# A fused attention and MLP kernel whose planner gets its first 400 operations as a list

## The chip, the cores and the metric

One NeuronCore of a Trainium2 chip runs the whole program. The metric is the device time of one execution in microseconds (us), given as the median of several runs. A profiled execution of the kernel before is shown beside them; every instant below counts from the first instruction of that profile.

## The reference

Two computations follow each other. First, attention with a causal window of 64 positions, over 8 batches, 8 heads, 576 positions and a head size of 64:

```
scores = q @ k.T / sqrt(64)                  # only 0 <= i - j < 64 counts
attn   = exp(scores - max) / (sum + 1e-9)
a      = attn @ v
```

Its result is laid out as x with 4608 tokens (8 x 576) of 512 features. Second, an MLP with a gate of its own:

```
h   = x @ w_in                               # 4608 x 2048
g   = h * clip(h + 3, 0, 6) / 6
out = g @ w_out                              # 4608 x 512, float32
```

## The kernel before

The MLP works on tiles of 512 tokens, 9 of them. Stage 1 of a tile makes 16 chunks of h, each of four 128x512 matmuls (`s1_part`, recorded as L736; one matmul for each pair of heads g, since x is made pair by pair); ScalarE (ACT) applies a relu with bias (L749) and VectorE (DVE) multiplies (L754). Stage 2 makes four output blocks of 128 tokens, each with 16 matmuls (`s2_part`, L775); ACT or DVE copies the finished block out of PSUM (`s2_close`, L788) and SyncE (SP) stores it.

Between those matmuls stands the attention of the next batch, so that x is ready when its tile begins. For a batch this is: the loads of q, k and v by GpSimd's DMA queue (POOL, L389); the turning of q and k so that the head size lies along partitions (for batches 0 and 1 on TensorE, `fold_pair` and `fold_two`, L513 and L539, with copies out of PSUM, L518 and L544; later by two DMA transposes on SP, `turn`, L391); the scores (L580; for batch 0 with a mask added by a matmul, L564), the exp on ACT (L596), the mask on DVE (L605); and the product with v. For batches 0 and 1 that product has the queries along partitions (`pv_rows`, L625), is divided by its row sum on DVE (L635, L636) and turned back by TensorE (`turn_x`, L651, then a copy, L368). For later batches (`pv`, L677) the sums come out as rows, and ACT makes the reciprocal as exp(-ln(sum)): two LN instructions (L683) and one EXP (L686) for each of five products of a batch (four pairs of heads and "e", the last 64 positions of all pairs). Two DVE multiplies (L697) then write x and free the PSUM bank.

v is wanted in two alignments. For batch 0, pairs 0 and 1 come through a float32 stage loaded by SP in four pieces of 128 positions, and six copies cast it to bf16 (`cast_v`, L368): for the blocks 0 and 1 the straight piece and two pieces shifted by 64 positions, then the same for blocks 2 and 3. Pairs 2 and 3 are loaded as bf16 by POOL (`load_vhead`), and `shift_v` (L456) makes the shifted parts. `copy_op` and `shift_v` may go to any of several engines.

Every engine takes its instructions in the order in which the program emits them, and that order comes from a planner that runs while the program is built. `Plan.add` notes each operation with a duration, its reads and writes; the operation's number (`op.seq`) is its place in that list. `Plan.solve` picks one operation after another, the one that could start first by its own account (a preference for each stream is subtracted), gives it an engine, a start and an end, and PSUM banks: there are five slots, two "n" of one bank, one "b" and two "a" of two banks. At the end all operations are emitted in the order of their planned starts. A result counts as usable by another engine `LAT` ns after the operation's end. For the first loads of each queue the planner doesn't work out the landing but takes it from the tables `LANDED` (SP, POOL, ACT) and `NEXT` (POOL's following ones):

```
op.done = max(op.land or ring[eng] + 600 + op.late, t + dur)
```

with `op.land` the entry of the table (for NEXT, plus `MARGIN`), t the planned issue and dur the issue's own duration. `COLD_PE` is the time up to which TensorE counts as 1.6 times slower. Matmuls on ones (L977) are put ahead of the first TensorE operation, as many as fit before its planned start.

The numbers that matter below:

| number | operation |
|---|---|
| 3, 5 / 10 | casts of q and k of pair 0 / ACT's table load |
| 11-19 | POOL: loads of q and k of the pairs 1 to 3 of batch 0, identity, mask |
| 20, 21 / 22, 23 | POOL: load_vhead, pairs 2 / 3 of batch 0 |
| 24, 25 | DVE: fold and ident, from the identity |
| 26, 27, 28 / 29, 30, 31 | cast_v, blocks 0-1 / 2-3: straight, shifted, shifted |
| 32-36 | POOL: the five loads of w_in (chunks 0-1, 2-3, 4-7, 8-11, 12-15) |
| 37-40 | shift_v of the pairs 2 and 3 |
| 85, 86, 91, 92 | POOL: the four loads of w_out |
| 88, 89 / 93, 94 | POOL: q and k of batch 1, pairs 0-1 / 2-3 |
| 162 | first TensorE operation that needs the last quarter of w_out |
| 203-210 | shift_v of batch 1 |
| 223, 227, 231 | pv_rows of batch 1, pairs 0, 1, 2 |
| 255, 256 | SP: turn of q, of k of batch 2 |
| 165, 167, 177, 179 | SP: the stores of the first four output blocks |
| 323, 329 | s2_close of the output blocks 5 and 6 |
| 353, 359, 365, 371, 377 | pv of batch 2: pairs 0, 1, e, 2, 3 |
| 354-356, 360-362, 366-368, 372-374, 378-380 | their LN, LN, EXP on ACT |
| 357-358, 363-364, 369-370, 375-376, 381-382 | their multiplies on DVE |
| 406-408 | first matmuls of tile 2's stage 1 (408 is the first on pair 3) |

## Time and profile before

| what | value |
|---|---|
| median of 3 runs (lowest, highest) | 300.72 us (300.55, 301.58) |
| the profiled execution: its own time, its span | 299.92 us, 298.2 us |
| granted TensorE clock | 0.999 |
| busy: TensorE (PE), DVE, ACT, POOL | 287.4, 198.6, 207.6, 121.7 us |
| POOL's DMA queue (q0) | 98816 packets, 17.80 MB |
| HBM read, written | 36.70 MB, 9.44 MB |

The span runs from the first to the last instruction; 1.72 us of the execution's time lie outside of it. Busy time of an engine counts instructions and not their waits on semaphores; matmuls are pipelined, and their ends are modelled, so consecutive starts tell more of TensorE than its busy share. "Released by" in a view is inferred from semaphores.

### The profile page before, as it was taken

The page shows a single profiled execution, that of the slowest core. Times are in us where ns is not written, and L with a number is a line of the kernel's source. Part 1 is how long each engine was busy: PE and PEld are TensorE (multiplying, and loading weights), DVE is VectorE, ACT ScalarE, POOL GpSimd, SP SyncE. Part 2 cuts the span into 40 slices and gives each one's busy share as a digit, 9 for nine tenths or more (in the row PEclk, how much of TensorE's full clock was granted, in tenths as well). Part 3 has the DMA queues.
Part 4 walks back from the last instruction along what each step waited for, and adds up shares of the span by engine and source line. Part 5 has one row for each costly group of instructions (what it writes and reads, how often), then busy time and mean ns, then how long its engine had stood idle before and what let it go on. Part 6 is the DMA issues. An engine that isn't in the chain of part 4 may idle for free.

```text
span 298.2 us, 6931 instructions
## 1 busy us (share of the span) xinstructions
PE 287.4 (96%) x2779; PEld 153.7 (52%) x2825; DVE 198.6 (67%) x326; ACT 207.6 (70%) x323; POOL 121.7 (41%) x171
## 2 busy tenths in 40 slices
PE   6899999999999999999999999999999999999996
PEld 6544545445544554455687554455445544444443
DVE  3778657786777975878678767878677868106700
ACT  3878665887968795778677958886787768227611
POOL 8884667059547906930991069405000000000000
PEclk9999999999999999999999999999999999999999
DMA  8999999989999999999996799969900110110011
GB/s 186 189 208 205 204 190 169 192 93 152 129 210 147 114 155 177 181 64 208 137 169 41 143 178 170 71 110 173 118 2 35 37 70 1 37 70 35 0 73 70
DMA packets 137680, 36.66 MB, mean 123 GB/s; under 512 B 126256, under 2 KB 132912, under 8 KB 137648
## 3 DMA queue, kind: packets, MB, share of 16 engines
q0 software_dynamic: 98816, 17.80, 73.9%
q1 hardware_dynamic: 38688, 18.12, 24.8%
q8 instruction: 22, 0.36, 0.5%
q10 hardware_dynamic: 144, 0.29, 0.4%
q14 instruction: 10, 0.08, 0.1%
HBM read 36.70 MB, written 9.44 MB: 155 GB/s over the span
## 4 chain that ended last, share of the span: by engine, by line
PE 82%; DMA 11%; POOL 4%; issue 2%; ACT 0%; POOLq 0%
PE pn L775 36%; PE pn L736 16%; PE pa L736 12%; PE pb L736 9%; DMA Ak<-in_k_dram 7%; DMA wout<-in_moe_w_out_dram 4%; PE pa L677 4%; PE pa L580 2%; PE pa L775 1%; POOL nq L389 1%; PE pb L677 1%; POOL nk L389 1%; POOL Aq L389 0%; POOL V L456 0%; PE pb L580 0%
## 5 line engine op out<-in xcount | busy, mean ns | idle before, releaser
L775 PE MATMUL pn<-wout,gT 128*128 128x512 bf16 x532 | 125.3, 379 | 2.2 <-issue 1.1
L736 PEld LDWEIGHTS <-win 128*128 128x128 bf16 x640 | 62.0, 98 | 60.5
L775 PEld LDWEIGHTS <-gT 128*128 128x128 bf16 x592 | 54.3, 98 | 57.7
L736 PE MATMUL pn<-xT,win 128*128 128x512 bf16 (+1 forms) x271 | 62.0, 357 | 0.3
L749 ACT ACTIVATE t<-pn,half 128x512 bf16<-128x512 f32 x62 | 42.7, 689 | 8.8 <-PE pn L736 8.5
L754 DVE SCALAR_TENSOR_TENSOR gT<-t,pa 128x512 bf16<-128x512 bf16 x47 | 32.2, 687 | 24.2 <-ACT t L749 23.9
L754 DVE SCALAR_TENSOR_TENSOR gT<-t,pn 128x512 bf16<-128x512 bf16 x62 | 42.6, 687 | 8.6 <-ACT t L749 8.4
L736 PE MATMUL pa<-xT,win 128*128 128x512 bf16 (+1 forms) x201 | 47.8, 358 | 0.3
L389 POOL DMA_DIRECT2D nk<-in_k_dram x55 | 41.8, 790 | 5.3 <-DMA Tk<-nk 4.6
L389 POOL DMA_DIRECT2D V<-in_v_dram x40 | 33.2, 848 | 14.4 <-PE pa L677 11.9
L749 ACT ACTIVATE t<-pa,half 128x512 bf16<-128x512 f32 x47 | 32.2, 686 | 8.9 <-PE pa L736 8.5
L697 DVE TENSOR_TENSOR xT<-pa,rec 64x512 bf16<-64x512 f32 (+1 forms) x48 | 32.0, 667 | 8.6 <-ACT rec L686 7.6
L736 PE MATMUL pb<-xT,win 128*128 128x512 bf16 (+1 forms) x153 | 36.3, 357 | 0.5 <-issue 0.5
L754 DVE SCALAR_TENSOR_TENSOR gT<-t,pb 128x512 bf16<-128x512 bf16 x35 | 24.0, 686 | 16.2 <-ACT t L749 16.1
L788 ACT COPY osb<-pn 128x512 f32<-128x512 f32 x17 | 10.0, 586 | 32.2 <-PE pn L775 32.2
L683 ACT ACTIVATE rec<-pa 64x512 f32<-64x512 f32 (+1 forms) x48 | 27.6, 574 | 4.8 <-PE pa L677 3.7
L749 ACT ACTIVATE t<-pb,half 128x512 bf16<-128x512 f32 x35 | 24.2, 690 | 7.6 <-PE pb L736 7.5
L389 POOL DMA_DIRECT2D nq<-in_q_dram x30 | 26.8, 892 | 3.3 <-DMA wout<-in_moe_w_out_dram 1.6
L596 ACT ACTIVATE pT<-pa 128x1024 bf16<-128x1024 f32 x25 | 24.6, 1021 | 1.5 <-PE pa L580 1.3
L605 DVE TENSOR_TENSOR pT<-pT,mask 128x1024 bf16<-128x1024 bf16 x28 | 18.9, 689 | 4.8 <-ACT pT L596 4.8
L677 PEld LDWEIGHTS <-V 128*128 128x128 bf16 x448 | 16.9, 98 | 6.8 <-DVE xT L697 0.5
L853 POOL COPY scrap<-Tq 128x1 bf16<-128x1 bf16 x5 | 0.9, 189 | 44.4 <-DMA Tq<-nq 44.4
(96 smaller groups left out, 205.9 us busy)
## 6 DMA issues: line engine op xcount, KB each, us to landing
out_dram<-osb SPq DMA_DIRECT2D x35, 256.0 KB, 3.6
V<-in_v_dram POOLq DMA_DIRECT2D x28, 128.0 KB, 5.9
nq<-in_q_dram POOLq DMA_DIRECT2D x24, 128.0 KB, 4.7
nk<-in_k_dram POOLq DMA_DIRECT2D x41, 64.0 KB, 4.2
wout<-in_moe_w_out_dram POOLq DMA_DIRECT2D x4, 512.0 KB, 14.5
win<-in_moe_w_in_dram POOLq DMA_DIRECT2D x3, 512.0 KB, 9.2
V<-in_v_dram POOLq DMA_DIRECT2D x12, 64.0 KB, 5.8
Aq<-in_q_dram POOLq DMA_DIRECT2D x2, 288.0 KB, 13.7
```

Of the source, the lines that this page charges most:

```text
L389: em = lambda: e.dma_start(out=out_ap, in_=in_ap)
L580: nc.tensor.matmul(to[o, home(b, g, h) if x == "e" else h, y * D : (y + 1) * D], lhsT=w, rhs=q_cols(b, r, g, j), start=not masked, stop=no ...
L596: nc.scalar.activation(out=p_[:].rearrange("p j h c -> p h j c"), in_=wide(add_far if masked else op, name)[:, :, 0 : n * D].rearrange("p ...
L605: nc.vector.tensor_tensor(out=pp, in0=pp, in1=mask[:, m0 : m0 + n, :, :].rearrange("p j h c -> p (j h c)"), op=MULT)
L677: nc.tensor.matmul(wide(op, name)[:, h, y * D : (y + 1) * D], lhsT=V[:, blk, g, h * D : h * D + P], rhs=p_[:, y, home(b, g, h) if end else ...
L683: add("ACT", act(n), lambda h=h: nc.scalar.activation(out=rc[rows[h], 0:n], in_=wide(op, name)[rows[1 - h], h, 0:n], func=LN), reads=[key] ...
L697: nc.vector.tensor_tensor(out=o, in0=a, in1=z, op=MULT)
L736: nc.tensor.matmul(bank(op, name)[:, to : to + n], lhsT=win16[:, g, fc * P : (fc + 1) * P], rhs=xT[:, g, o : o + n], start=(g == 0), stop= ...
L749: nc.scalar.activation(out=t1[ti][:], in_=bank(op, name), func=RELU, bias=half[:], scale=1.0 / 6.0)
L754: nc.vector.scalar_tensor_tensor(out=gT[:, fc, :], in0=t1[ti][:], scalar=1.0, in1=bank(op, name), op0=MIN, op1=MULT)
L775: nc.tensor.matmul(bank(op, name)[:, 0:n], lhsT=gT[:, fc, col : col + P], rhs=wout16[:, fc, js], start=(fc == 0), stop=(fc == NFC - 1))
L788: alts = {e: (f(n), (lambda e=e: cpy(e)(out=osb[oi][:, js], in_=bank(op, name)[:, 0:n])), False) for e, f in (("DVE", dve), ("ACT", act))}
```

## The change

It gives `Plan.solve` a list, `PLACE`, of 400 operation numbers. While fewer than 400 operations are placed, the next one of the list is the only candidate; where an operation may go to several engines, the next letter of `WHERE` (D, A, P for DVE, ACT, POOL) tells which. From the 401st on the planner picks as before. Besides: the tables `LANDED` and `NEXT` get other times, `MARGIN` goes from 300 to 0 and `COLD_PE` from 6500 to 4500; `LAT` becomes a table by the engine that made the result, with 20 for a landed DMA; the price of an ACT operation falls from 160 + n/1.2 to 75 + n/1.2 ns, that of a DVE copy within SBUF from 60 + 0.9 n to 60 + 0.73 n; and in `pv` both multiplies, not the last alone, count as holders of the PSUM bank.

```diff
--- before.py
+++ after.py
@@ -21,13 +21,34 @@
 
 WINDOW = 64
 LANDED = {
-    "SP": (3000, 6210, 8070, 8430, 9600),
-    "POOL": (4600, 6820, 7920, 9640, 10900, 11600, 11950, 12350, 12800, 13200),
-    "ACT": (3200,),
+    "SP": (4255, 4660, 6885, 8395, 10180,),
+    "POOL": (5370, 7235, 8520, 9515, 10470, 11545, 11850, 12265, 12700, 13150,),
+    "ACT": (4285,),
 }
-NEXT = (15140, 16470, 19010, 21590, 24580, 26640, 29180, 30650, 32050, 32490, 35020, 37600, 39010, 40440, 41280, 42170, 43000, 43830, 44270, 45500, 46500, 47500, 48500, 49500, 50500, 51500, 52500, 53300, 54000)
-MARGIN = 300
-COLD_PE = 6500
+NEXT = (14470, 15805, 18450, 21875, 24250, 26720, 29260, 30705, 32120, 32620, 35100, 37660, 39100, 40510, 41370, 42225, 43055, 44245, 45105, 46465, 47585, 48465, 49295, 50140, 50975, 51850, 52770, 53125, 54155,)
+PLACE = (
+    0, 11, 2, 12, 13, 14, 4, 6, 15, 16, 18, 25, 3, 19, 20, 21, 7, 24, 41, 5, 48, 43, 42, 8,
+    44, 17, 45, 50, 10, 49, 26, 51, 46, 52, 55, 53, 57, 47, 59, 27, 1, 9, 29, 28, 30, 54, 31, 69,
+    62, 22, 56, 58, 70, 23, 60, 64, 63, 73, 38, 65, 32, 61, 66, 74, 40, 37, 33, 67, 68, 75, 77, 39,
+    78, 34, 35, 71, 36, 85, 81, 86, 76, 82, 72, 79, 102, 87, 103, 88, 89, 83, 90, 91, 92, 80, 93, 84,
+    106, 105, 107, 108, 111, 94, 104, 95, 109, 117, 112, 110, 96, 118, 113, 97, 114, 120, 119, 181, 121, 182, 126, 123,
+    98, 127, 128, 122, 99, 100, 135, 115, 136, 132, 116, 129, 144, 124, 137, 130, 125, 131, 138, 183, 145, 133, 134, 139,
+    147, 141, 140, 148, 150, 142, 101, 146, 149, 153, 156, 143, 154, 191, 151, 157, 192, 180, 155, 193, 184, 152, 194, 158,
+    195, 196, 159, 211, 214, 212, 185, 161, 160, 162, 186, 163, 197, 190, 187, 164, 198, 168, 189, 215, 188, 200, 199, 202,
+    169, 201, 245, 246, 247, 213, 216, 166, 219, 248, 220, 221, 203, 172, 205, 170, 171, 204, 208, 207, 222, 217, 206, 223,
+    231, 227, 173, 224, 249, 228, 225, 210, 174, 229, 232, 209, 226, 218, 235, 233, 230, 175, 250, 251, 234, 263, 252, 236,
+    178, 237, 239, 264, 176, 238, 240, 253, 265, 268, 271, 241, 269, 270, 274, 266, 267, 272, 165, 273, 255, 280, 167, 242,
+    277, 177, 275, 276, 254, 243, 278, 244, 283, 279, 281, 179, 256, 286, 282, 284, 289, 285, 287, 292, 288, 290, 295, 291,
+    293, 298, 294, 296, 301, 297, 299, 304, 300, 302, 257, 307, 303, 258, 305, 310, 306, 259, 308, 341, 309, 260, 311, 342,
+    313, 312, 261, 344, 262, 314, 343, 383, 345, 346, 384, 315, 347, 385, 349, 348, 316, 386, 351, 319, 350, 387, 320, 317,
+    388, 352, 338, 321, 337, 389, 340, 339, 353, 390, 359, 354, 391, 365, 322, 355, 392, 360, 318, 325, 323, 356, 393, 326,
+    361, 357, 394, 362, 327, 358, 395, 366, 363, 371, 367, 396, 328, 364, 368, 397, 372, 369, 324, 377, 373, 370, 331, 329,
+    378, 374, 332, 398, 379, 375, 333, 380, 376, 334, 381, 406, 335, 382, 407, 330, 408, 411, 399, 409, 414, 412, 410, 417,
+    400, 415, 401, 413, 420, 418, 402, 416, 423,
+)
+WHERE = "DAAADDDPDPPPADADADPDAAAAADDADAAAADAPDAPDPAAAAAADAAADADAAA"
+MARGIN = 0
+COLD_PE = 4500
 FAR = 8.0e9
 
 
@@ -52,7 +73,7 @@
 
 
 
-    LAT = 150
+    LAT = {"PE": 150, "ACT": 150, "DVE": 70, "POOL": 70, "SP": 20}
     LAG = 3000
     NSLOT = {"n": 2, "b": 1, "a": 2}
     TURN = {("f", "r"): 95, ("r", "f"): 95, ("f", "c"): 95, ("c", "f"): 220, ("r", "c"): 100, ("c", "r"): 100}
@@ -137,10 +158,13 @@
             for a in op.frees:
                 holds.setdefault(a, []).append(op)
         order = []
+        where = iter(WHERE)
         while left:
             best = None
-            for key, lst in streams.items():
-                cands = lst[:1] if key in inorder else lst[:24]
+            n = len(order)
+            placed = n < len(PLACE)
+            at = next(where) if placed and self.ops[PLACE[n]].alts else None
+            for cands in [[self.ops[PLACE[n]]]] if placed else [lst[:1] if k in inorder else lst[:24] for k, lst in streams.items()]:
                 for op in cands:
                     if any(d.start is None for d in op.deps) or any(d.start is None for d in op.follows):
                         continue
@@ -160,9 +184,11 @@
                         continue
                     pick = None
                     for eng, (dur, emit, port) in (op.alts or {op.eng: (op.base, op.emit, op.port)}).items():
+                        if at and eng[0] != at:
+                            continue
                         t = max(free.get(eng, 0.0), ts)
                         for d in op.deps:
-                            lat = 0 if d.eng == op.eng and eng == "PE" else self.LAT
+                            lat = 0 if d.eng == op.eng and eng == "PE" else self.LAT["SP" if d.packets else d.eng]
                             t = max(t, d.done + lat)
                             if op.stream == "st":
                                 t = max(t, d.done + self.LAG)
@@ -209,7 +235,7 @@
                 nlane[eng] += 1
             for a in op.frees:
                 holds[a].remove(op)
-                until[a] = max(until.get(a, 0.0), op.done + self.LAT)
+                until[a] = max(until.get(a, 0.0), op.done + self.LAT[op.eng])
                 if not holds[a]:
                     s, kind = slot_of.pop(a)
                     slot_free[kind][s] = until[a]
@@ -351,7 +377,7 @@
         return max(n / 2.4 + 2.5, 29.0)
 
     def act(n):
-        return 160 + n / 1.2
+        return 75 + n / 1.2
 
     def dve(n, fast=1):
         return 150 + n / 0.96 / fast
@@ -363,7 +389,7 @@
         return {"DVE": nc.vector.tensor_copy, "ACT": nc.scalar.copy, "POOL": nc.gpsimd.tensor_copy}[eng]
 
     def copy_op(n, out_ap, in_ap, engines, reads, writes, sbuf=False, prio=0, after=()):
-        cost = {"DVE": dve(n) if not sbuf else 60 + n * 0.9, "ACT": act(n), "POOL": pool(n)}
+        cost = {"DVE": dve(n) if not sbuf else 60 + n * 0.73, "ACT": act(n), "POOL": pool(n)}
         src = in_ap if callable(in_ap) else lambda: in_ap
         alts = {e: (cost[e], (lambda e=e: cpy(e)(out=out_ap, in_=src())), sbuf) for e in engines}
         stream = "ACT" if "ACT" in engines else engines[0]
@@ -698,7 +724,7 @@
 
             e = add("DVE", dve(n), ml, reads=[key, ("rc", ri, h)],
                     writes=[("x", b % RB, g, 1 if end else 0, h) for g in gs], prio=pr + 100)
-        e.frees = (name,)
+            e.frees = (name,)
         return op
 
 
```

## Prediction

> **What bounds the kernel now.** I read the page first, then TensorE's waits, its timeline, the DMA view by stretches, and last the timelines of POOL, DVE and ACT where the new order differs.
>
> ```profile
> PE 287.4 (96%) x2779; PEld 153.7 (52%) x2825; DVE 198.6 (67%) x326; ACT 207.6 (70%) x323; POOL 121.7 (41%) x171
> PE   6899999999999999999999999999999999999996
> ```
>
> TensorE is full from the third of 40 slices on. In its timeline the first stage 1 matmul starts at 16.3 us; from there consecutive 128x512 matmuls start every 216 ns, and what exceeds that is about 0.1 us at each change between wide and narrow matmuls, plus a few waits. So the end moves only by what TensorE loses or gains. Its waits in the whole span:
>
> ```profile
> PE pn L977 <- DVE ones L857: 1.1, 1, 1.1
> PE pn L513 <- DVE Aq L368: 0.9, 1, 0.9
> PE pn L651 <- DVE opg L636: 0.5, 1, 0.5
> PE pa L625 <- POOL V L456: 0.4, 1, 0.4
> ```
>
> The first three are before 16.3, the last at 45.8. A second bound runs beside TensorE. This is the DMA view for 10 to 43 us:
>
> ```profile
> DMA  9999999999999999999999999999999999999999
> q0 software_dynamic: 13250, 6.38, 145.6%
> ```
>
> POOL's queue moves some 200 GB/s without a hole. So a load lands when the bytes ahead of it are through, and TensorE follows closely. The last quarter of w_out, then the matmuls of which the sixth, at 37.77 (36.69 + 5 x 0.216), is the first to read it:
>
> ```profile
> L389 POOL DMA_DIRECT2D wout<-in_moe_w_out_dram x1: 747/747/747, 21.6 to 21.6; - x1
> DMA to landing us min/median/max: 15.9/15.9/15.9
> ...
> 36.69 2.97 PE L775 MATMUL pn<-wout,gT 128*128 128x512 bf16 x12
> ```
>
> Issued at 21.65, landed at 37.58: 0.19 us of slack. By the same view others have more: w_in 4-7 lands at 18.79 (used 19.97), batch 1's first q at 30.64 (31.61), its last k at 40.43 (40.97). So nothing won before 38 us can count for more than 0.15 unless the stream itself is earlier; a later stream counts nearly in full.
>
> **Part 1: the stream.** The list leaves POOL alone up to load 21, then puts the casts 27, 28, 30, 31 ahead of loads 22 and 23 and of w_in.
>
> ```profile
> 5.94 3.00 POOL L389 DMA_DIRECT2D V<-in_v_dram  x4
> 9.28 2.31 POOL L389 DMA_DIRECT2D win<-in_moe_w_in_dram  x3 [0.34 <-DMA Aq<-in_q_dram]
> 10.12 0.95 DVE L368 CAST V<-stage 128x512 bf16<-128x512 f32 x2 [0.61 <-DMA stage<-in_v_dram]
> ```
>
> Cast 31 reads the last staged piece of v, which lands at 10.1 (third line: DVE waits for it today). On POOL everything behind waits for that too. No row shows this cast on POOL; its f32-to-bf16 casts of the mask take 0.29 (128 columns) and 0.94 (896), a line that gives 0.62 for 512; bounds 0.53 (the shift copy) and 0.94. With 0.74 for each issue: cast 31 from 10.11 to 10.73, load 22 at 10.73 (today 7.42), 23 at 11.47, first w_in at 12.21 (9.28), shift 37 to 13.53, second w_in at 13.53. How long from issue to first packet? After an idle queue, in slices of 0.2 us from 62:
>
> ```profile
> DMA  0000000000000259999999999999999999999999
> ...
> 63.04 4.21 POOL L389 DMA_DIRECT2D V<-in_v_dram  x5 [0.41 <-DVE gT L754]
> ```
>
> The packets begin at 64.65, 1.61 after the issue (1.61 to 1.63 in three other restarts, over 3 in two where transposes or stores held the DMA engines). So w_in's first bytes move at 13.82; they need 1.34 (the distance of the first two w_in landings, 14.70 and 16.04) and 0.9 from last packet to landing (load at 63.04, landed 66.47, with 0.85 of packets): 16.06 instead of 14.70. The second is issued in time to follow at once, so from there the queue is full again and everything to 43 us is 1.35 late. The planner can't see this: a table entry replaces its landing whatever the issue time. At 37.8 TensorE then waits 1.35 - 0.15 = **+1.2**. Bounds: 0 if today's backlog swallowed the late issues, 1.6 with the dearer cast. [...]
>
> **Part 2: before 16.3.** The fold identity (24) comes behind q's cast, so the first turn starts some 0.2 later (DVE row 0.23). ACT's table load, idle-time work at 1.24 today (1.28 long), moves between k's first copy and the first exp: that exp starts at 8.7 instead of 7.52. Following the rows, exp of pair 2 ends at 14.1 (13.17), of pair 3 at 15.05 (15.39), and the first stage 1 matmul comes at 16.3 to 16.4: **0**, bounds -0.4 and +0.6. The stream's 1.2 hides either; without that cover the cost stands. [...]
>
> **Part 3: 43 to 53.** pv_rows of pair 0 starts at 45.73, stops for POOL's shift and goes on at 46.36. POOL now makes three shifts (203, 208, 206) instead of five, ACT the other one of pair 0, done before TensorE comes: -0.5. Pairs 0, 2, 1 run in a row (223, 231, 227), two mode changes less: -0.2. Sum **-0.7**, bounds -0.9 and 0 (v's rows, landing at 45.2 with the late stream, are then the next wait). On SP the turn of q now stands ahead of the stores 167 and 177; they wait some 12 us for its loads, nobody waits for them, and the turn of k behind them slips 0.7 (two issues of 0.36) from its landing at 62.3, needed at 65.7: 0.
>
> **Part 4: 74 to 85.** WHERE sends the copies 323 and 329 from DVE to ACT.
>
> ```profile
> 74.46 1.20 ACT L683 ACTIVATE rec<-pb 64x512 f32<-64x512 f32 x2 [0.88 <-PE pb L677]
> 75.68 0.59 ACT L683 ACTIVATE rec<-pa 64x512 f32<-64x512 f32 x1
> 76.17 0.62 ACT L686 ACTIVATE rec<-rec 128x512 f32<-128x512 f32 x1
> ...
> 82.34 0.63 ACT L686 ACTIVATE rec<-rec 128x512 f32<-128x512 f32 x1
> 83.15 1.39 DVE L697 TENSOR_TENSOR xT<-pa,rec 64x512 bf16<-64x512 f32 x2
> 84.96 0.38 PE L736 MATMUL pa<-xT,win 128*128 128x512 bf16 x1
> ```
>
> ACT's fifteen instructions fill 74.46 to 82.97 without a hole; then DVE multiplies to 84.54, and matmul 408 reads x at 84.96: slack 0.4. 323 goes in behind 360 and 329 behind 373, both ahead of the last EXP: 2 x 0.59 (L788's row) = 1.2 later. So 1.2 - 0.4 = **+0.8** of TensorE's waiting, first 0.5 of it at 78.4, where pair 2's product takes the bank that the multiplies of pair 0 free at 78.23 today, 0.6 later then. Bounds +0.6 (copies overlapping as others do, 0.49 apart) and +0.8; 0 only if ACT's chain had air.
>
> **Part 5: the rest.** From operation 401 the planner orders with new prices. It counts 502 ns for a 512-column ACT operation; the rows of the chain above come every 0.6. So it believes chains 0.1 per instruction too short, over a dozen in each of five more batches. In tile 3 the bank is free at 107.40 and pair 2's product comes at 107.67; in later tiles the slack is 1.0 to 1.1. I count one stall, **+0.3**; bounds -0.2 (there is hardly a wait left to win) and +3.0 (0.6 in each of five).
>
> Sum: +1.2 + 0 - 0.7 + 0.8 + 0.3 = +1.6. It is made against the profiled execution (299.92: span 298.2 and 1.72 around it); the median of the runs is 0.80 above that, so **302.3**.
>
> **Rivals.**
> - *On the other side: the landings hold.* If the queue's backlog at 7 to 12 us covers the late issues, TensorE reaches 38 us 0.15 earlier, loses the wait at 45.8 and two mode changes: -0.85, and -0.95 with 0.1 of the small waits, at 299.8. It decides by load 22's first packet: 11.6 or earlier. For it: loads 20 to 23 take 5.5 to 6.2 us today, so there is backlog. Against: load 21's packets end at 11.6, and an issue at 10.73 can't show packets before 12.3. It also needs ACT's two copies to cost nothing. 0.20.
> - *Landings hold, ACT's copies bite:* -0.85 + 0.8 + 0.3 = +0.25, 301.0, no measurable change. 0.16.
> - *Stream late, copies hidden:* +1.2 - 0.7 = +0.5, 301.2, no measurable change. 0.12. [...]
> - *The new prices bite in every later batch:* the forecast's first 90 us (+1.3) and 0.3 to 0.6 in each of five tiles, +2.8 to +4.3, about 304.2. For it: PV products that follow a bank within 0.3 us. Against: slack over 1.0 in four tiles. 0.10.
>
> That the list would not act is no rival: on each engine the planned starts grow along it, and the emission sorts by them.
>
> **How the numbers follow.** A measurement here tells about 0.3% (0.9 us) from no change. The forecast (+1.6) has 0.42, together with the last rival 0.52 slower; the two middle cases 0.28 same; the first 0.20 faster. The range, 299.6 to 304.2, takes in the first rival's 299.8 and half of the last one's cases; the forecast's own is 301.7 to 303.0.
>
> **What the profile after would show.** Part 1: the first w_in issue near 12.2 and a landing near 16; the w_out wait of TensorE near 38 us. Part 3: no wait of L625 for POOL. Part 4: fifteen LN and EXP with two L788 among them and a PE gap before pair 3 of tile 2. Part 5: gaps ahead of L677 in tiles 3 to 7. Landings as today, or a stage 1 start well before 16 with landings to match, would prove me wrong.

## The result, and the profile after

| | before | changed |
|---|---|---|
| median of 6 runs, us | 300.84 | 308.13 |
| lowest to highest, us | 300.55 to 301.58 | 306.36 to 308.8 |
| profiled execution, us (its span) | 299.92 (298.2) | 308.8 (307.1) |

The changed kernel takes 1.0235 times as long (95% interval 1.0207 to 1.0263). The direction was forecast; the size was not: 302.3 stood on record, with 304.2 as the upper end. Lines of the changed kernel are 26 higher than those of before (L625 is L651, L677 is L703, and so on). One execution in each of three experiments took far longer than all the others (1066, 1475 and 342 us) and is left out of the ratios. The changed kernel's list holds 417 operations, not the 400 that the text above says; nothing below rests on that.

The page of the changed kernel: busy times, and the bars of TensorE and of its granted clock.

```profile
PE 295.6 (96%) x2839; PEld 156.2 (51%) x2839; DVE 192.3 (63%) x317; ACT 212.9 (69%) x332; POOL 123.6 (40%) x172
...
PE   8799999998699999999999999999999999999996
...
PEclk9879999999999999999999999999999999999999
```

TensorE is no less full than before (96%), but its 295.6 us of "busy" hold 8 us more than before for the same products (some 3 of the 8 are no lost time: the profile before lacks 28 of the 560 stage 2 matmuls); in slices 2 and 3 (8 to 23 us) the clock digit falls to 8 and 7, and slices 10 and 11 (69 to 84 us) of TensorE's bar have an 8 and a 6 where before had nines. So there are two places to look at: 8 to 30 us, and 65 to 84 us. The list of TensorE's waits names both:

```profile
PE pb L703 <- ACT V L482: 2.3, 1, 2.3
PE pa L651 <- POOL V L394: 1.5, 1, 1.5
...
PE pa L606 <- DMA Tk<-nk: 1.0, 1, 1.0
PE pn L762 <- DMA win<-in_moe_w_in_dram: 0.7, 1, 0.7
```

The second and fourth line lie before 25 us, the third at 70 and the first at 81.6 us. To see what each is worth, the starts of the same work on TensorE are read off the two timelines (its first weight load or matmul, whichever is first):

| work on TensorE | before | changed | later by |
|---|---|---|---|
| first stage 1 work of tile 1 (its weight load) | 16.23 | 19.32 | 3.1 |
| batch 0's product for its last 64 positions | 32.70 | 37.94 | 5.2 |
| batch 1, pair 0's pv_rows | 45.73 | 50.85 | 5.1 |
| turning back batch 1's pair 0 | 48.35 | 52.91 | 4.6 |
| scores of batch 2 | 65.73 | 71.50 | 5.8 |
| batch 2, pair 1's product with v | 74.23 | 82.02 | 7.8 |
| batch 2, pair 2's product with v | 78.29 | 86.78 | 8.5 |
| a stage 1 chunk of the next tile | 84.96 | 93.69 | 8.7 |
| span | 298.2 | 307.1 | 8.9 |

Five of the nine microseconds are lost by 33 us, 0.5 come back around 50, some 4.2 are lost between 53 and 94, and then almost nothing happens any more.

*The first loss.* POOL's timeline in the changed kernel:

```profile
11.77 0.61 POOL L394 CAST V<-stage 64x512 bf16<-64x512 f32 x1 [2.28 <-DMA stage<-in_v_dram]
12.32 1.49 POOL L415 DMA_DIRECT2D V<-in_v_dram  x2
13.80 0.76 POOL L415 DMA_DIRECT2D win<-in_moe_w_in_dram  x1
14.60 0.61 POOL L482 COPY V<-V 64x512 bf16<-64x512 bf16 x1
15.16 2.97 POOL L415 DMA_DIRECT2D win<-in_moe_w_in_dram  x4
```

The cast that reads the last staged piece of v ends at 12.38; behind it loads 22 and 23 go out at 12.32 (7.42 before) and the first of w_in at 13.80 (9.28). Then shift 37 holds the queue once more until 15.16. What the stream makes of it is seen in the busy times of three stretches of 2 us (after the five engines come TensorE's granted clock, the DMA engines' share and, last, GB/s), first in the kernel before, then in a second profile of the changed kernel:

```profile
12.00:14.00 2.00, 1.95 (x71) 1.54 (x66) 1.68 (x4) 1.85 (x3) 1.69 (x3) 1.00 1.59 190
14.00:16.00 2.00, 1.47 (x52) 1.09 (x52) 1.93 (x5) 1.61 (x3) 2.00 (x4) 1.00 1.37 210
16.00:18.00 2.00, 1.90 (x14) 1.15 (x16) 1.61 (x3) 1.24 (x3) 1.96 (x4) 1.00 1.23 201
```

```profile
12.00:14.00 2.00, 1.81 (x63) 1.36 (x63) 1.40 (x4) 1.35 (x3) 1.96 (x4) 1.00 1.04 66
14.00:16.00 2.00, 1.68 (x41) 1.21 (x42) 0.61 (x1) 2.00 (x3) 2.00 (x4) 1.00 1.16 142
16.00:18.00 2.00, 0.78 (x18) 0.51 (x17) 1.72 (x6) 0.74 (x2) 2.00 (x3) 0.93 1.07 136
```

From 190 to 210 the rate has fallen to 66 to 142, although in that second profile the loads go out again from 10.85 on. The first w_in load lands at 18.35 in the first profile (14.70 before), the third at 23.97 (18.79), the last quarter of w_out at 42.85 (37.58).

*The second loss.* On SP the turn of q now stands first, and its stores come out behind it:

```profile
59.55 3.10 SPq L417 DMA_TRANSPOSE Tq<-nq  x1
62.76 1.49 SPq L415 DMA_DIRECT2D out_dram<-osb  x3
64.47 3.67 SPq L417 DMA_TRANSPOSE Tk<-nk  x1
```

Before, one store of 0.55 stood between the two turns, and the turn of k was issued at 57.27 and landed 5.05 later. Here three stores of 1.49 stand there, and the turn lands at 71.46, 7.0 after its issue (the experiment on SP's order, below, tells what makes it longer). POOL's loads of v for batch 2 are queued behind a copy that waits for that turn, ACT's V shift waits for those loads, and TensorE, two matmuls into pair 0's product, for that shift:

```profile
81.63 0.58 PE L703 MATMUL pb<-pT,V 128*128 128x64 bf16 x14 [2.31 <-ACT V L482]
```

### The profile page after: what moved, and what is told of

Read it like the earlier page. It is cut to its first block, busy times and chain, and to the rows that moved or that the text cites. A ratio compares the mean times of both kernels' runs of the same rounds, so it can differ in the third digit from the quotient of the medians.

```text
span 307.1 us, 6990 instructions
## 1 busy us (share of the span) xinstructions
PE 295.6 (96%) x2839; PEld 156.2 (51%) x2839; DVE 192.3 (63%) x317; ACT 212.9 (69%) x332; POOL 123.6 (40%) x172
## 4 chain that ended last, share of the span: by engine, by line
PE 70%; DMA 14%; POOL 5%; issue 3%; ACT 3%; DVE 2%; SPq 1%; POOLq 0%
PE pn L801 31%; PE pn L762 13%; PE pa L762 10%; PE pb L762 8%; DMA wout<-in_moe_w_out_dram 4%; DMA V<-in_v_dram 3%; DMA stage<-in_v_dram 3%; PE pa L703 3%; DMA Tk<-nk 2%; DVE xT L723 2%; PE pa L606 2%; POOL V L415 2%; PE pa L801 1%; DMA nk<-in_k_dram 1%; POOL V L482 1%
## 5 line engine op out<-in xcount | busy, mean ns | idle before, releaser
L801 PE MATMUL pn<-wout,gT 128*128 128x512 bf16 x560 | 128.3, 379 | 0.0
L762 PE MATMUL pn<-xT,win 128*128 128x512 bf16 (+1 forms) x280 | 64.3, 358 | 0.7 <-DMA win<-in_moe_w_in_dram 0.7
L762 PE MATMUL pa<-xT,win 128*128 128x512 bf16 (+1 forms) x212 | 48.8, 359 | 0.1
L762 PE MATMUL pb<-xT,win 128*128 128x512 bf16 (+1 forms) x148 | 34.6, 356 | 0.0
L814 ACT COPY osb<-pn 128x512 f32<-128x512 f32 x24 | 14.0, 582 | 28.5 <-PE pn L801 28.5
L723 DVE TENSOR_TENSOR xT<-pa,rec 64x512 bf16<-64x512 f32 (+1 forms) x44 | 29.2, 665 | 5.6 <-ACT rec L712 4.7
L780 DVE SCALAR_TENSOR_TENSOR gT<-t,pb 128x512 bf16<-128x512 bf16 x33 | 22.6, 686 | 13.3 <-ACT t L775 13.3
L709 ACT ACTIVATE rec<-pa 64x512 f32<-64x512 f32 (+1 forms) x44 | 25.2, 573 | 5.5 <-PE pa L703 4.5
L775 ACT ACTIVATE t<-pb,half 128x512 bf16<-128x512 f32 x33 | 22.8, 689 | 7.0 <-PE pb L762 7.0
L703 PEld LDWEIGHTS <-V 128*128 128x128 bf16 x448 | 16.0, 98 | 9.1 <-ACT V L482 2.4
```

The source lines that it names most:

```text
L703: nc.tensor.matmul(wide(op, name)[:, h, y * D : (y + 1) * D], lhsT=V[:, blk, g, h * D : h * D + P], rhs=p_[:, y, home(b, g, h) if end else ...
L709: add("ACT", act(n), lambda h=h: nc.scalar.activation(out=rc[rows[h], 0:n], in_=wide(op, name)[rows[1 - h], h, 0:n], func=LN), reads=[key] ...
L723: nc.vector.tensor_tensor(out=o, in0=a, in1=z, op=MULT)
L762: nc.tensor.matmul(bank(op, name)[:, to : to + n], lhsT=win16[:, g, fc * P : (fc + 1) * P], rhs=xT[:, g, o : o + n], start=(g == 0), stop= ...
L775: nc.scalar.activation(out=t1[ti][:], in_=bank(op, name), func=RELU, bias=half[:], scale=1.0 / 6.0)
L780: nc.vector.scalar_tensor_tensor(out=gT[:, fc, :], in0=t1[ti][:], scalar=1.0, in1=bank(op, name), op0=MIN, op1=MULT)
```

## The experiments

The edits are edits of the list: the order of an engine, or the letter of an operation; one also takes out a rule of the program, as said there. Ratios are to the kernel before, run beside the experiment on the same chip, with their 95% interval. From one such set of runs to the next the median of the kernel before moves between 300.14 and 300.84 us, so a time in us is compared across sets only by its distance to that median.

### The changed kernel once more

```diff
 (no edit)
```

> The changed kernel itself once more, for a second profile. In the first one the last staged piece of v landed at 11.7 (9.6 to 10.1 in every other kernel run so far) and TensorE's clock stood at 0.5 from 12 to 19. Theory (both belong to this list): the piece lands near 11.7 again, clock 0.5 again, 307.5 to 308.5. Rival (that landing is a draw of that execution): it lands near 10, the clock stays at 1.00, load 22 is issued near 10.6, and the time is still over 306, by the queue's drain alone.

307.51 us (306.55 to 308.57), ratio 1.024 (1.0214 to 1.0267). The rival holds for the landing and the time: the last piece came at 10.24, and load 22 went out at 10.85. Its clock of 1.00 did not come.

```profile
10.29 0.61 POOL L394 CAST V<-stage 64x512 bf16<-64x512 f32 x1 [0.96 <-DMA stage<-in_v_dram]
10.85 1.50 POOL L415 DMA_DIRECT2D V<-in_v_dram  x2
12.32 0.77 POOL L415 DMA_DIRECT2D win<-in_moe_w_in_dram  x1
```

These are the issue times that the prediction worked out (10.73 for load 22, 12.21 for w_in, 13.53 for the second w_in load, measured 13.69). And yet the first w_in load landed at 16.95, the third at 22.54, the second quarter of w_out at 33.81: 2.3, 3.8 and 4.6 later than before. So the loss doesn't come from the late landing of the piece in the first profile. The clock did fall, but only from 17.7 to 21.1 us. Of the changed kernel's first six executions two had a mean granted clock of 1.00; they took 308.55 and 306.36. The half clock is no condition of the loss. The rival's cause, the queue's drain, is taken up by the next three experiments.

### Casts back on DVE; shift 37 back behind the loads; both

```diff
 casts 27, 28, 30, 31 (letters)
-P P P P
+D D D D
```

> The changed kernel with the four casts of v (27, 28, 30, 31) back on DVE, nothing else of the list altered. Theory (the casts hold POOL's queue, so the loads behind them are issued late and TensorE pauses at 10.6): load 22 is issued near 7.5 again, the first w_in lands near 14.7, stage 1 starts near 16.3 at a granted clock of 1.00, and 4 to 5 us of the 7.3 come back: 303 to 304. Rival (the staged pieces of v themselves land late, 11.7 against 10.1, for a reason that lies in the rest of the list): the pause at 10.6 and the half clock stay, w_in is early, and only 1 to 2 us come back: 306 to 307.

307.0 us, ratio 1.0226 (1.0201 to 1.0251): the theory missed. The time is the rival's (306 to 307), but not for its reason: neither its pause at 10.6 nor its half clock is there. In the profiled execution the clock stands at 1.00, load 22 goes out at 7.57, the first w_in load lands at 15.08, and yet the time is only 0.4 nearer to the kernel before (6.9 us above it, against 7.3). POOL's timeline tells why:

```profile
13.06 0.61 POOL L482 COPY V<-V 64x512 bf16<-64x512 bf16 x1 [2.60 <-DMA V<-in_v_dram]
13.62 2.96 POOL L415 DMA_DIRECT2D win<-in_moe_w_in_dram  x4
```

Shift 37 waits 2.6 us for v's landing, and the second w_in load behind it goes out at 13.62 (10.01 before). It lands at 17.32 and the third only at 22.89. One hold of the queue has taken the place of the other; this wait of the shift stood in neither theory.

```diff
 POOL's order (changed list, casts left on POOL)
-22, 23, 32, 37, 33, 34, 35, 36
+22, 23, 32, 33, 34, 35, 37, 36
```

> The changed kernel with loads 33, 34, 35 ahead of POOL's shift 37 again, the casts left on POOL ahead of load 22. Theory (the casts hold the queue until 12.3 already; the shift adds its own 0.6 behind them): at most 0.7 us come back, 307.4 to 308.2. Rival (the shift is the larger hold even behind the casts): 2 us or more, 306 or less.

305.17 us, ratio 1.0153 (1.0129 to 1.0177): the theory missed, the rival was right (2 us or more). The shift is 0.6 long and waits for nothing here, but taking it out from between the w_in loads is worth 2.3 us (over the second run of the changed kernel) to 2.6 (by the distance to the kernel before). The first w_in load lands no earlier (17.61), but the next come at distances of 1.72, 2.56 and 2.53, as before the change (1.34, 2.75, 2.57), where the second profile of the changed kernel has 1.96, 3.63 and 3.67.

```diff
 both edits: POOL's order
-27, 28, 30, 31, 22, 23, 32, 37, 33, 34, 35, 36
+22, 23, 32, 33, 34, 35, 37, 36
```

> The changed kernel with the four casts on DVE and, besides, loads 33, 34, 35 ahead of POOL's shift 37 again, as before the change. Theory (two holds of POOL's queue in a row, first the casts until 12.3, and, with these gone, shift 37 until 13.6, each of them enough to drain the queue): with both undone w_in lands at 14.7, 16.0, 18.8, 21.4, 24.3 as before, TensorE is within 1 us of before up to 43, and 4 to 5 us of the 7.3 come back: 303 or less. Rival (the late third landing of the run with the casts on DVE, 22.9, has another cause than the hold, such as slower packets): that landing stays over 20 and less than 1 us is won over that run: 306 or more.

302.67 us, ratio 1.0068 (1.0042 to 1.0093): theory. w_in lands at 15.12, 16.45, 18.99, 21.58 and 24.09, the last quarter of w_out at 37.59 (37.58 before). 5.1 of the 7.3 us are back (2.2 left above the kernel before). That the loss at the start is the two holds of POOL's queue is shown: each taken away alone gave 0.4 and 2.6 back, the two together 5.1; with either one left the stream is still late.

### The constants alone, and the casts put into the order of before

The order and the engines of the kernel before, written as a list, with the new constants for all that follows:

> The order and engines of the kernel before for the first 400 operations, written as a list, and the new plan constants for all that follows: the constants alone. Theory (part 5 of the prediction was right to be small): within 0.5 us of the kernel before, 300.3 to 301.3. Rival (the new prices cost something in each later batch): 302.0 or more, with new waits of TensorE after 96 us.

300.09 us against 300.14 in the same set, ratio 0.9991 (0.9972 to 1.001). The constants are free.

```diff
 POOL's order (list of before)
-20, 21, 22, 23, 32, 33, 34, 35, 37
+20, 21, 27, 28, 30, 31, 22, 23, 32, 33, 34, 35, 37
```

> The order and engines of the kernel before for the first 400 operations, written as a list, with the one difference that the four casts of v run on POOL ahead of load 22; the new constants are in for what follows. To be read against the same list with the casts on DVE (e5). Theory (held queue plus TensorE's pause and low clock): 3 to 5 us over e5, first w_in landing near 18, TensorE's clock near 0.5 for some us before 18. Rival (the sum on record: only a late stream): 1.2 us over e5, first w_in landing near 16.

303.23 us, ratio 1.0098 (1.0078 to 1.0118), 3.1 over the run with the constants alone: the theory's lower end. Load 22 goes out at 10.66, w_in lands at 17.53, 18.88, 21.71, 24.25. In the profiled execution the clock stays at 1.00, against the theory's sign of a half clock (of its four executions one, at 303.25 us, had a mean clock of 0.994 and took no longer). So this is the price of the held queue and of TensorE's short pause, without any fall of the clock.

```diff
 POOL's order (list of before)
-20, 21, 22, 23, 32, 33, 34, 35, 37
+20, 21, 27, 28, 30, 22, 23, 32, 33, 34, 35, 37
```

> The list of the kernel before with casts 27, 28 and 30 on POOL ahead of load 22, cast 31 (which waits for the last staged piece) on DVE: a hold that ends about 9.4 instead of 10.7 with all four (303.23) or 7.6 with none (300.09). Theory (a hold costs only from the point where the queue drains; the record put it at a first packet of load 22 at 11.6, which is an issue at 10.0): load 22 is issued near 9.5, w_in lands at 14.5 to 15.0, third landing under 19, within 0.5 of the list without casts on POOL: 299.8 to 300.6. Rival (each us of hold costs, 3.1 us for 3.0 of hold): 301.5 or more.

302.07 us, ratio 1.0057 (1.0038 to 1.0075): the theory missed, the rival was right. Load 22 goes out at 9.20 instead of 7.64, so that by 1.61 from issue to first packet its packets were due at 10.8, before those of load 21 end (11.6). Even so the rate from 12 to 14 us is 123 GB/s against 190, the first w_in load lands at 15.43 (14.52 with none of the casts on POOL), the third at 20.11 (18.45). What makes it slow is shown in part. Loads 22 and 23 move 64 KB each and are issued 0.74 apart, so their issue alone allows some 88 GB/s (an estimate from these two numbers; in the run before 88 were measured from 12 to 14 us). The first w_in load, issued at 10.66, was due at 12.3 by 1.61, yet the rate is 81 GB/s from 12 to 13 and only then 165. A hold of 1.6 us cost 2.0 by the run with the constants alone, 1.4 by the kernel before of its own set; a hold of 3.0 cost 3.1.

```diff
 POOL's order (list of before, all four casts on POOL)
-27, 28, 30, 31, 22, 23, 32, 33, 34, 35
+27, 28, 30, 31, 32, 33, 22, 23, 34, 35
```

> The list of the kernel before with all four casts on POOL ahead of the loads (303.23), and now the first two w_in loads (512-byte packets) ahead of v's loads 22 and 23 (128-byte packets). Theory A (a drained queue moves whatever comes next more slowly, 64 to 90 KB/us against 151 for v and 125 to 150 against 200 for w_in): the second quarter of w_out, 31.9 with v first, lands at 31.3 to 32.3 again; 302.5 to 304. Theory B (only v's small packets are slow, since each of their loads takes 0.74 of issue for 0.43 of packets): w_in's packets move at 195 to 200 KB/us from their start, that landing comes at 30.5 or earlier, and the time is 302 or less.

This edit also takes out the rule of the program by which the first w_in load has to follow loads 22 and 23.

304.44 us, ratio 1.0133 (1.0109 to 1.0158), theory A. The second quarter of w_out lands at 31.84, where v first gave 31.88. From 12 to 14 us, nearly all of it w_in's packets, 144 GB/s move, against 190 before and 88 with v first. So v's small packets make it worse, but w_in's are slow too after the hold. Why they are is not shown. (The 0.7 to 1.2 us over the run with the same four casts on POOL and v first come with v: pair 3's rows land at 18.16, and TensorE waits 3.3 for the last normalised block. Its clock also stood at 0.5 from 19.54 to 22.95, so the two are not told apart.)

### TensorE's pause without a held queue

```diff
 POOL's order (changed list)
-27, 28, 30, 31, 22, 23, 32, 37, 33, 34, 35, 36
+22, 23, 32, 27, 28, 30, 31, 37, 33, 34, 35, 36
```

> The changed kernel with the four casts still on POOL, but loads 22, 23 and the first w_in load issued ahead of them. Theory A (what costs is the held queue): w_in lands near 14.7 to 15.5 and 3.5 us or more come back: 305 or less. Theory B (what costs is TensorE's pause for cast 31 and the low clock after it): the pause is as long or longer, the clock is near 0.5 until about 18 to 20, and stage 1 is late although its weights are there: less than 2 us come back, 306 to 308.

Ratio 1.0222 (1.0178 to 1.0266), three times between 305.64 and 308.21. It has no trace that could be read beside the others, so neither theory is settled; shift 37, which still stood ahead of load 33, would have blurred it anyway. The next one takes that hold out as well:

```diff
 POOL's order (changed list)
-27, 28, 30, 31, 22, 23, 32, 37, 33, 34, 35, 36
+22, 23, 32, 33, 34, 35, 27, 28, 30, 31, 37, 36
```

> The changed kernel with the casts still on POOL, but behind loads 22, 23 and the first four of w_in (32 to 35): no queue hold at all, while TensorE has to wait for the casts until about 13.7, over 2.5 us. Against 302.67 (the same queue, casts on DVE). Theory A (the queue is what counted; a pause of TensorE costs only its own length beyond the slack of the first stage): w_in lands at 15.1 to 24.3, and 303.5 to 304.5. Theory B (a pause of over 2 us lets the granted clock fall to 0.5 for some 7 us, as in the profile of the changed kernel): clock near 0.5 from 13 to 20, and 305.5 or more.

> Once more the changed kernel with its casts on POOL behind loads 22, 23 and 32 to 35 (305.31), for the profile, since the one execution that was recorded of it had taken 1475 us. Theory A (the pause of TensorE costs its own length): granted clock 1.00 from 10 to 20, first stage 1 matmul at 18 to 18.5, w_in landings as with the casts on DVE. Theory B (the pause lets the clock fall): clock near 0.5 for some 7 us after the pause, first stage 1 matmul after 19.

305.31 and, the second time, 305.22 us (ratios 1.0165 and 1.0161, the second from 1.0139 to 1.0183). The second one's trace is read here. w_in lands at 14.63 to 23.65, earlier than before the change, so the queue costs nothing here. TensorE's timeline, where the product of pair 0 waits twice for POOL's casts:

```profile
10.58 0.26 PE L651 MATMUL pa<-V,pT 128*64 128x65 bf16 x4
13.79 0.26 PE L651 MATMUL pa<-V,pT 128*64 128x65 bf16 x4 [2.96 <-POOL V L394]
15.12 0.44 PE L651 MATMUL pa<-V,pT 128*64 128x65 bf16 x8 [1.08 <-POOL V L394]
```

and the stretches behind it (granted clock in the third column from the end):

```profile
15.00:18.00 3.00, 2.88 (x77) 2.50 (x77) 1.22 (x4) 1.26 (x3) 2.90 (x6) 0.50 1.25 207
22.00:24.00 2.00, 1.95 (x14) 0.93 (x12) 0.70 (x2) 1.17 (x2) 0.68 (x1) 1.00 1.25 207
```

The clock falls to 0.5 at 14.92 and is back at 21.75. The first stage 1 work starts at 21.84, 4.8 after that of the run with both holds undone. Of these, 3.3 are longer waits for casts (4.0 against 0.7); the other 1.5, an estimate by difference, are left for the half clock. At the scores of batch 2 the distance is still 4.5. It then shrinks to 2.7, since that run has a wait of 1.6 at 75 us that this one doesn't have: its turn of k for batch 2 lands 5.4 after its issue, with the same three stores ahead, that run's after 7.1 (more below). Theory A's price was too low, theory B's clock was right and its time a little too high. So here a pause of TensorE in the first stage is about as dear as a late stream. That the two don't add up is likely but not fully shown: of the changed kernel's ten executions, where the stream is late, three at full clock took 306.36, 306.55 and 308.55 us, the seven with a lower mean clock 307.38 to 308.8; but no two experiments have the pause with and without the late stream and all else the same.

### The two later orders

```diff
 SP's order (both holds undone)
-165, 255, 167, 177, 179, 256
+165, 167, 177, 255, 179, 256
```

> The changed kernel with both early holds undone (casts on DVE, loads 33 to 35 ahead of shift 37) and, of the two later orders, SP's alone as before: the turn of q (255) behind the stores 167 and 177; POOL's shifts 203, 208, 206 stay ahead of the loads 249 to 251. Between 302.67 (neither order undone) and 301.24 (both). Theory (the turn of q at SP's head holds the stores, the stores then meet the transposes, Tk lands late and with it the V loads and ACT's shift): 300.5 to 301.3, no wait of TensorE for ACT's V shift near 75. Rival (POOL's shifts, which stand in front of the nq and nk loads, make it late): 302.3 or more, the wait still 1.6.

301.06 us, ratio 1.0037 (1.0016 to 1.0059): theory. 302.67 without this edit has a ratio of 1.0068 to the same 300.49. In the run with both holds undone the wait of TensorE was there although the stream was on time,

```profile
PE pb L703 <- ACT V L482: 1.6, 1, 1.6
```

and with SP's order as before it is gone. POOL's copy that waits for Tk, with the loads of v behind it, without and with the edit:

```profile
66.16 0.19 POOL L879 COPY scrap<-Tk 128x1 bf16<-128x1 bf16 x1 [14.93 <-DMA Tk<-nk]
66.75 4.22 POOL L415 DMA_DIRECT2D V<-in_v_dram  x5 [0.41 <-DVE gT L780]
```

```profile
63.14 0.19 POOL L879 COPY scrap<-Tk 128x1 bf16<-128x1 bf16 x1 [11.78 <-DMA Tk<-nk]
63.74 4.22 POOL L415 DMA_DIRECT2D V<-in_v_dram  x5 [0.41 <-PE pa L762]
```

Three microseconds: one from the issue of the turn of k (58.93 against 57.97), two from its own time to landing, 7.1 with three stores directly ahead and 5.05 with one. The stores alone don't make these two. In the trace with the casts behind w_in (the second run of it) the same three stores stand directly ahead, and the turn lands after 5.4. The DMA view from issue to landing, without the edit and then in that trace:

```profile
q1 hardware_dynamic: 2910, 1.21, 73.4%
q8 instruction: 1, 0.02, 0.8%
issues: line engine op xcount, KB each, median us to landing
Tk<-nk SPq DMA_TRANSPOSE x1, 7.1
```

```profile
q1 hardware_dynamic: 2916, 1.22, 95.4%
issues: line engine op xcount, KB each, median us to landing
Tk<-nk SPq DMA_TRANSPOSE x1, 5.4
```

The difference is one 16 KB packet of q8, a fetch of instructions. In all five traces with a turn of 7.0 to 7.1 such a packet begins 4.9 to 5.1 after the issue and takes 0.9; fifteen of the turn's sixteen DMA engines have reported by 5.5, and the last packet of SP's queue ends only with or just after that fetch. With one store ahead the queue's last packets end 4.5 to 4.6 after the issue, before any fetch begins (4.86 or later). So the stores cost some 0.4, and they move the turn's end into a fetch that costs some 1.6 more. That it is the fetch is read from its time in these traces; no run was made to test it.

```diff
 and POOL's order
-248, 203, 208, 206, 249, 250, 251, 252
+248, 249, 250, 251, 203, 208, 206, 252
```

> The changed kernel with both holds undone (casts on DVE, loads 33 to 35 ahead of shift 37), and with two orders of 43 to 65 us as before: on SP the turn of q (255) behind the stores 167 and 177, on POOL the loads 249 to 251 ahead of the shifts 203, 208, 206. Theory (those two orders make Tk late, then the V loads, then ACT's V shift that TensorE waits for near 82): against the run without these two, another 1.5 to 3 us, 299.5 to 301. Rival (that chain was late only because the first stream was): within 0.6 us of the run without them.

301.24 us, ratio 1.002 (1.0004 to 1.0036): the theory's 299.5 to 301 just missed, and 1.4 less than with both holds undone instead of 1.5 to 3. SP's order explains all of it; POOL's adds nothing that can be told apart from the run above. In its trace the shifts, now behind three loads, make TensorE wait 0.5 at batch 1's pv_rows again.

### The two copies

```diff
 closes 323, 329 (letters), on top of the run above
-A A
+D D
```

> As the run with both holds and both orders undone, and the closes 323 and 329 back on DVE. Theory (part 4 of the prediction): 0.5 to 0.9 us less than that run, and no gap of TensorE before pair 2's and pair 3's products of tile 2. Rival (copies hidden): within 0.3 us of that run.

300.37 us, ratio 1.0002 (0.9984 to 1.002), 0.87 less than the run above, in the same set. Theory. With these edits (casts, shift 37, SP, POOL, copies) the changed list is level with the kernel before.

### The start of before, the middle of the changed list

The first 190 operations in the order and on the engines of the kernel before; from there the changed list with SP's order and the letters of 323 and 329 as before.

> The order and engines of the kernel before up to the start of batch 1's pv_rows (190 operations), from there the changed list, but with SP's order and the engines of closes 323 and 329 as before: what is left of the change is part 3 (pairs 0, 2, 1 in a row, POOL's three shifts) and the new constants. Theory (part 3 is worth -0.5 to -0.9, the constants nothing): 299.2 to 299.8, and no wait of L651 for POOL near 46. Rival (the order of 43 to 53 gives back on POOL what it wins on TensorE): 300.0 to 300.8.

299.68 us (12 runs), ratio 0.9976 (0.996 to 0.9992): theory. It beats both kernels, the one before by 0.24%. From one and the same stage 2 block (162) to the turning back of pair 0 its TensorE needs 9.85 us (38.64 to 48.49), the kernel before 10.79 (37.56 to 48.35). The interval of the constants alone (0.9972 to 1.001) overlaps with this one, so that by total time the two are not told apart.

## Why the prediction was wrong, and where it was right

**The step that failed** is in part 1: "The second is issued in time to follow at once, so from there the queue is full again and everything to 43 us is 1.35 late." The mechanism before it was right: casts on POOL, cast 31 waits for the staged piece, loads 22, 23 and w_in behind it, issue times right to 0.16 us (second profile). But it priced the late start alone and let the stream run at its old rate from the first packet. By the stretches above the stream moved 2 x (66 + 142 + 136) = 688 KB from 12 to 18 us, before 2 x (190 + 210 + 201) = 1202. With 117 against 156 from 10 to 12 and 158 against 207 from 18 to 20 some 690 KB are missing, 3.4 us at 205. The rest to the 4.6 us of the second quarter of w_out lies in the landing, which is the last of the sixteen completion writes that the traces show for a load: they spread over 2.96 us instead of 1.55 for that load (the last one 1.15 after the fifteenth), over 2.2 instead of 1.3 for the third w_in load; in the first profile over 2.3 and 2.5. The upper bound of 1.6 was made from the price of the cast and so could not hold this. The term was +1.2; it measured about +5 (5.2 by 33 us in the profile; 5.1 with both holds undone). Why the packets come slower after the hold stays open; v's are held back in part by their issue, w_in's are not (256 KB every 0.73 us). In the first profile TensorE also paused 1.5 us and ran at half clock from 12.29 to 19.12. The prediction has neither; both lie under the late stream there.

**The rival "the landings hold"** had its point of decision at a first packet of load 22 by 11.6. The short hold kept to that (due at 10.8) and still cost 1.4 to 2.0 us: the point was wrong too. It asked only for load 22. Load 23 and the first of w_in, issued at 9.93 and 10.66, come behind it at the distances of their issues, and from 12 to 13 us the rate is 81 GB/s.

**Shift 37** was seen (a second w_in load at 13.53) and called harmless, by the same step. It is the larger part of the two.

**Part 2** said 0 (bounds -0.4 and +0.6). With both holds undone the first stage 1 work comes at 17.06, 0.8 late, for TensorE waits 0.7 for DVE's cast of v; slightly over the bound, and hidden under the stream in the changed kernel, as said. The table load stands where it was put:

```profile
7.78 1.28 ACT L891 ACT_TABLE_LOAD   x1
9.07 1.02 ACT L622 ACTIVATE pT<-pa 128x1024 bf16<-128x1024 f32 x1
```

The first exp begins 10 ns after the load's end. ACT also carries a second table load, at 1.23 ahead of its first copy, in idle time.

**Part 3** said -0.7 on TensorE. Measured: -0.6 in the changed kernel (5.1 late at pair 0's pv_rows, 4.6 at its turning back) and -0.9 in the last experiment. The size was right; its sign, "no wait of L625 for POOL", did not come (0.3 in the changed kernel, none only in the last experiment). **Its sentence on SP failed**: "the turn of k behind them slips 0.7 (two issues of 0.36) from its landing at 62.3, needed at 65.7: 0". It counted two issues and TensorE as the only user. The issue slipped by 0.96, the stores added some 0.4 to the turn and the fetch beside its end some 1.6; and POOL's queue for v stands behind a copy of its result, with ACT's shift behind that: before, this shift ended at 73.57 and pair 0's product started at 73.58, with no slack at all. Price: 1.6 us (302.67 to 301.06) with the stream on time, 3.3 in the changed kernel, where the scores waited 1.0 and the product 2.3. How much of it would be left without the fetch is not shown.

**Part 4** said +0.8, first 0.5 and then 0.3. The copies measured 0.87 by their own experiment, and 0.7 and 0.24 at pair 2's product and the next tile in the changed kernel. Right.

**Part 5** said +0.3. The constants alone cost -0.05, and the changed kernel loses 0.2 from 94 us to the end. The size was within its bounds, the one stall that was counted isn't there.

So of a forecast of +1.6, the terms of 43 to 53 us, of the copies and of the constants stood; +1.2 for the stream should have been +5, and 0 for SP +1.6 or more. By the experiments the 7.3 us above the kernel before are 5.1 (both holds) + 1.6 (SP) + 0.9 (copies), and 0.3 that the changed list wins elsewhere, which is within the noise. No run shows what the upper bound of +0.6 in part 2 and 301.7, the lower end of the forecast's own range, stand on; measured were +0.8 for part 2 without the late stream and about +5 for the stream.

## What to carry to other kernels

An instruction put ahead of DMA issues on the engine that issues them cost about the time for which it held the loads back, or more: here 1.4 to 2.0 us for a hold of 1.6, 3.1 for one of 3.0, and 2.3 to 2.6 for a copy of 0.6 that waited for nothing. Behind the hold the queue ran slower for some 6 us (66 to 142 GB/s from 12 to 18 us in the second profile of the changed kernel, 190 to 210 before the change). Price it by rates in the stretches after a restart, not by the shift of one issue time. Follow a slipped transfer through everything that is queued behind its consumer (here turn, POOL copy, v loads, ACT shift, product), and read the slack at the last of them. Look at the last completion of a transfer, too, and not only at its bytes: in the changed kernel fifteen of the sixteen completions of the turn of k were there 5.44 us after its issue, the last one, and with it the landing, came at 6.99. When one hold is taken away, look for the next one before the theory is given up: here the casts alone gave back 0.4 us and both holds 5.1.

## What was not expected of the hardware

- A queue of POOL that had run thin moved 66 to 142 GB/s for some 6 us (12 to 18) where a backlogged one moved 190 to 210, with loads issued 0.73 us apart. The stretches don't hold the same packets. By size, those of 128 bytes moved at 63 to 101 GB/s instead of 150, those of 512 bytes at 101 to 168 (137 to 178 with w_in first) instead of 195. For v's loads, of 64 KB, the issue alone sets a bound near 88, an estimate from 64 KB every 0.74 us; for w_in's, of 256 KB, it doesn't, and why those are slower is not shown by any run.
- The first packet after the hold came 1.47 us after its issue in the first profile, 1.46 in the second and 1.45 with the casts on DVE (1.61 in the restarts that the prediction read).
- The turn of k for batch 2 took 5.0 to 5.1 us to land with one store issued right before it, 5.4 with three, and 7.0 to 7.1 with three and a 16 KB fetch of instructions beside its end, by one late completion write of sixteen.
- The granted clock fell to 0.5 after pauses of TensorE at the start: from 12.29 to 19.12 and from 17.74 to 21.15 in the two profiles of the changed kernel, from 14.92 to 21.75 with the longest pause, from 19.54 to 22.95 with w_in ahead of v. The lengths are 6.8, 3.4, 6.8 and 3.4 us. In the profiled executions with the casts on DVE it did not fall, though TensorE waited up to 2.0 us at a time (for the third w_in load). In other executions of those kernels it did fall: one of four with the casts alone moved had a mean clock of 0.994 (the mean of the traces with one spell of 3.4 us), and in the run with the two copies on DVE again two of ten had 0.994 and 0.989 and took 301.45 and 301.81 us, the other eight 300.25 to 300.64. Which pause halves it is not shown.
